# Attention and two feed-forward layers on one core: start-up loads, late coefficients and the planner's search changed together

## Chip, cores and metric

One core of a Trainium2 chip. The metric is the device time of one execution in microseconds; less is better.

## What is computed

Attention over 4 batches of 12 heads (448 positions, 64 wide), with q and k normalised by their root mean square and scaled by gains, then two feed-forward layers without a residual. The first has a cosine in it, the second a quotient of polynomials whose coefficients (moe2_a, moe2_b) are inputs.

```
q_n, k_n = rmsnorm(q, g_q), rmsnorm(k, g_k)
attn = softmax(q_n @ k_n.T / sqrt(64));  x = attn @ v        # -> 1792 tokens x 768
h = x @ w_in;   x = (h * cos(h)) @ w_out                     # 768 -> 2048 -> 768
h = x @ w_in2;  P = a0 + a1 h + a2 h^2 + a3 h^3;  Q = 1 + |b0||h| + |b1| h^2
out = (P / (Q + 1e-6)) @ w_out2
```

The weights (and a, b, and all else) arrive as 8-byte floats; the kernel takes the 4-byte value out of their bits itself.

## The kernel before, in words

**Work.** Heads go in pairs, 6 pairs per batch, 24 in all. For one pair, `att_load` loads k (three DMAs) and q (four) into the tile qk, `att_norm` squares, sums and scales them, `att_t` transposes both on PE (eight 128x128 matmuls against the identity) and copies them to kt and qt as a high and a low half; `att_s` makes the scores in four chunks (tiles t), of which DVE takes the maximum (mx) and ACT the exponential (e) with its sums; `att_vt` transposes e to et, and `att_va` multiplies et by v into x_ps. The inverse sums go to all partitions either through DRAM (rd, rb) or, in batch 0, by `att_rows`, which transposes broadcast columns on PE. The result x is again stored as high and low halves, since each fp32 product in the feed-forward layers is three single-pass products (hi hi, hi lo, lo hi).

A weight block of 768 KB is decoded by `decode`: a load (raw) on SP's queue, three passes on DVE (tiles w32), a copy on ACT (high half) and a subtraction on POOL (low half), then a store to DRAM (wd), from which `load_w` takes it later. Blocks in the list `early` are decoded ahead and only stored; the others are kept in the ring w as well.

**Stages.** Batch 0's attention runs alone up to about 105 us. Then, batch by batch, the first layer (tiles h_ps, the nonlinearity on tiles k and g in `act1`, the sum y) runs with the next batch's attention between its groups. In the last stage the second layer runs over all tokens.

**Order.** Nothing is scheduled on the chip. `Clock` is a model of the engines: `do` enters a task with an engine, a duration and the tasks that it needs; `step` starts tasks; `pe` advances the time of TensorE, in whose program order the kernel is written. `candidate` picks the next task of an engine by due time. Each of 40 rehearsals runs the kernel without emitting anything, and `plan` derives new due times from it; the best set is then used to emit the instructions. Within each engine they run strictly in the order in which they were emitted. Work outside the model (`gains`, `consts`, `coefficients`) is emitted where it is called.

All engine calls go through a recording helper, so nearly every row of the profile carries the line L293 (L330 in the changed kernel). Names of tiles tell the rows apart.

The `coefficients` call stands in `run` after batch 0's attention, directly ahead of the first nonlinearity:

```
            self.moe1_part(0, f, c, KD - 1 - c)
            self.h_done[0, f] = KD - 1
        self.coefficients(const_p)
```

Of the kernel before, what the change touches and what calls it, by code (L numbers as in the profile page):

```python
# [29 lines left out]
REHEARSALS = 40  # L30
EXP, SIN = "natural_log_exp_and_others", "trig_and_small"


class Task:
    __slots__ = (
        "eng", "fn", "prio", "tab", "size", "ready", "left", "succ", "end", "out", "n",
        "port", "parts", "name", "due", "need", "lst", "start",
    )


class Clock:
# [4 lines left out]
    READ, WRITE, WINDOW = 2.2, 1.5, 3.413  # L46
# [3 lines left out]
    def __init__(self, due=None):  # L50
        self.t, self.n, self.named = 0.0, 0, {}
        self.free = dict.fromkeys(("V", "A", "G", "S"), 0.0)
# [5 lines left out]
        self.window, self.half = [0, 0.0], True  # L58

    def do(  # L60
# [15 lines left out]
        k.due = self.due.get(k.name, math.inf) if self.due else None  # L76
        self.all.append(k)
# [19 lines left out]
    def enter(self, k):  # L97
        for e in k.eng:
            self.todo[e].append(k)

# [11 lines left out]
    def candidate(self, e):  # L112
# [4 lines left out]

        def ready(k):
# [3 lines left out]
            return max(k.ready, rival) if k.port else k.ready  # L122
# [16 lines left out]
    def step(self, until=math.inf):  # L139
        best = None  # L140
        for e in self.free:
            c = self.candidate(e)
# [7 lines left out]
        if eng == "S":  # L150
# [3 lines left out]
        if len(k.eng) > 1:  # L154
            k.fn(eng)
        else:
            k.fn()
# [7 lines left out]
        if k.size:  # L165
            lag = self.READ if k.size > 0 else self.WRITE
            self.dma = max(self.dma, end - k.eng["S"] / k.parts + lag) + abs(k.size)
# [4 lines left out]
            end += self.LATE  # L172
# [33 lines left out]
    def pe(self, dur):  # L206


        while dur > 1e-9:
            n = int(self.t // self.WINDOW)  # L210
            if n > self.window[0]:
                idle, part = n > self.window[0] + 1, self.window[1] / self.WINDOW
                self.half = idle or part < (0.62 if self.half else 0.5)
                self.window = [n, 0.0]
            rate = 0.53 if self.half else 1.0
            d = min(dur / rate, (n + 1) * self.WINDOW - self.t + 1e-6)
            self.window[1] += d
            self.t += d
            dur -= d * rate
# [100 lines left out]
class Kernel:  # L320
    def __init__(self, tc, a, due):
        self.tc, self.nc, self.a = tc, Engines(tc), a
        self.dry = isinstance(tc, Null)
        self.ck = Clock(due)
# [34 lines left out]
    def gains(self, c):  # L359
        nc, a = self.nc, self.a  # L360
        g2 = c.tile([P, 2], F32, name="g2")
        for i, n in enumerate(("g_q", "g_k")):
            for r in HALVES:
                nc.gpsimd.dma_start(out=g2[r, i : i + 1], in_=a[n].rearrange("(p o) -> p o", o=1))
        return g2

    def consts(self, c, g2):
        nc, a = self.nc, self.a
        ident = c.tile([P, P + SL], F32, name="ident")
        if not self.dry:  # L370
            make_identity(nc, ident[:, :P])
        nc.gpsimd.tensor_copy(ident[:, P:], ident[:, :SL])
        self.ident, self.swap = ident[:, :P], ident[:, SL:]
# [14 lines left out]
        nc.vector.scalar_tensor_tensor(self.gg, g2[:, 0:1], 0.125, g2[:, 1:2], ALU.mult, ALU.mult)  # L388

    def coefficients(self, c):  # L390
        nc, a = self.nc, self.a
        ab = c.tile([P, 6], F32, name="ab")
        nc.gpsimd.dma_start(out=ab[:, 0:4], in_=a["moe2_a"].partition_broadcast(P))
        nc.gpsimd.dma_start(out=ab[:, 4:6], in_=a["moe2_b"].partition_broadcast(P))
        self.na = c.tile([P, 4], F32, name="na")
        nc.vector.tensor_scalar(self.na, ab[:, 0:4], -1.0, None, ALU.mult)
        self.bb = c.tile([P, 2], F32, name="bb")
        nc.scalar.activation(self.bb, ab[:, 4:6], AF.Abs)
# [1008 lines left out]
```

## Time and profile before

| what | value |
|---|---|
| median of three runs | 1278.93 us (1273.4, 1278.93, 1279.43) |
| the profiled execution, own time | 1273.58 us |
| its span | 1271.8 us |
| PE busy | 1232.2 us, 97% |
| DVE, ACT, POOL busy | 68%, 56%, 22% |
| HBM traffic over the span | 221 GB/s |

The span runs from the first to the last instruction of the profile; the time of an execution lies around it. PE is TensorE's matmuls, DVE is VectorE, ACT is ScalarE, POOL is GpSimd, SP issues most DMAs. A row's idle time is that of its engine just before it, with what ended it. The granted clock (PEclk) is given as a share of 2.4 GHz, the higher of the two levels; 0.50 is 1.2 GHz.

### The profile page before, as it was taken

What the parts mean: (1) busy time and instruction counts of PE and PEld (TensorE: products, weight loads), DVE (VectorE), ACT (ScalarE), POOL (GpSimd) and SP (SyncE); (2) the same over time, 40 slices, a digit from 0 to 9 for tenths busy, and PEclk for the clock granted to TensorE, in tenths of its full rate; (3) what the DMA queues carried; (4) which work ended last, traced back from release to release, by engine and by line L of the source; (5) the groups of instructions that cost most, each with busy time, mean ns of one, the idle gap of its engine ahead of it and who ended that gap; (6) DMA issues with size and microseconds to landing.
All of it is one profiled execution on the core that took longest, in us unless ns stands there. A gap on an engine that the chain in (4) does not pass through costs nothing.

```text
span 1271.8 us, 18275 instructions
## 1 busy us (share of the span) xinstructions
PE 1232.2 (97%) x6624; PEld 1055.3 (83%) x6624; DVE 860.4 (68%) x1360; ACT 710.0 (56%) x1373; POOL 273.6 (22%) x356
## 2 busy tenths in 40 slices
PE   5988999899999998999999999999999999999998
PEld 3557777678877878877879999999999999999998
DVE  6986886965766856776846556775766676577663
ACT  6875776563766654666554324675544455554540
POOL 5654354440424231324112111100000000000000
PEclk9999999999999999999999999999999999999999
DMA  5778786887797689798589999713141825142312
GB/s 129 219 241 288 239 291 194 269 277 267 245 324 266 200 288 352 274 307 303 190 312 369 403 367 364 263 69 149 50 151 50 333 101 199 50 149 88 120 42 87
DMA packets 132266, 282.24 MB, mean 222 GB/s; under 512 B 57424, under 2 KB 90448, under 8 KB 132176
## 3 DMA queue, kind: packets, MB, share of 16 engines
q1 hardware_dynamic: 131984, 281.06, 62.7%
q8 instruction: 53, 0.87, 0.3%
q14 instruction: 37, 0.30, 0.1%
q0 software_dynamic: 192, 0.00, 0.0%
HBM read 214.11 MB, written 66.91 MB: 221 GB/s over the span
## 4 chain that ended last, share of the span: by engine, by line
PE 80%; DMA 4%; DVE 2%; ACT 1%; issue 1%; POOL 1%; SPq 0%; DVEq 0%; POOLq 0%; ACTq 0%
PE h_ps L293 48%; PE o_ps L293 18%; PE t L293 9%; PE x_ps L293 4%; DMA w<-wd 3%; DMA raw<-in_moe_w_in 1%; DVE w L293 1%; DVE k L293 0%; DMA rb<-rd 0%; ACT k L293 0%; POOL w L293 0%; ACT w L293 0%; DVE x L293 0%; ACT L293 0%; SPq L293 0%
## 5 line engine op out<-in xcount | busy, mean ns | idle before, releaser
L293 PE MATMUL h_ps<-x,w 128*128 128x448 f32 x2250 | 488.2, 370 | 8.9 <-DVE qt L293 3.8
L293 PEld LDWEIGHTS h_ps<-x,w 128*128 128x128 f32 x2250 | 419.5, 189 | 54.7 <-issue 12.0
L293 PE MATMUL h_ps<-g,w 128*128 128x448 f32 x1152 | 248.2, 369 | 8.1 <-DVE k L293 6.2
L293 PE MATMUL o_ps<-w,g 128*128 128x384 f32 x1344 | 244.7, 337 | 0.0
L293 PEld LDWEIGHTS h_ps<-g,w 128*128 128x128 f32 x1152 | 213.6, 188 | 34.3 <-DVE k L293 8.4
L293 PEld LDWEIGHTS o_ps<-w,g 128*128 128x128 f32 x1344 | 237.1, 188 | 1.9
L293 DVE SCALAR_TENSOR_TENSOR w<-raw,w 128x768 int32<-128x768 int32 x128 | 139.7, 1095 | 1.1
L293 ACT ACTIVATE e<-t,mx 128x448 f32<-128x448 f32 x168 | 105.3, 637 | 33.3 <-DVE mx L293 33.1
L293 POOL TENSOR_TENSOR raw<-w,raw 128x768 fp32r<-128x768 f32 x40 | 74.9, 1874 | 211.8 <-ACT raw L293 200.4
L293 DVE TENSOR_REDUCE mx<-t 128x1 f32<-128x448 f32 x168 | 94.9, 613 | 7.5 <-PE t L293 7.1
L293 PEld LDWEIGHTS t<-ident,e 128*128 128x128 f32 (+1 forms) x696 | 76.5, 138 | 24.6 <-issue 20.6
L293 ACT ACTIVATE et<-t 128x512 f32<-128x512 f32 (+1 forms) x168 | 82.2, 554 | 25.4 <-PE t L293 25.1
L293 PE MATMUL t<-kt,qt 64*128 64x448 f32 (+1 forms) x504 | 84.6, 406 | 5.6 <-ACT e L293 4.3
L293 PE MATMUL x_ps<-et,v 128*64 128x448 f32 (+1 forms) x384 | 89.2, 560 | 0.2 <-ACT et L293 0.2
L293 PE MATMUL t<-ident,e 128*128 128x128 f32 (+1 forms) x696 | 88.6, 277 | 0.0
L293 ACT ACTIVATE g<-q 128x448 fp32r<-128x448 f32 x64 | 36.9, 577 | 89.7 <-DVE q L293 89.6
L293 PEld LDWEIGHTS t<-kt,qt 64*128 64x128 f32 (+1 forms) x504 | 51.6, 194 | 35.8 <-issue 16.1
L293 DVE SCALAR_TENSOR_TENSOR k<-k,h_ps 128x448 f32<-128x448 int32 x61 | 37.7, 619 | 57.2 <-ACT k L293 56.9
L293 ACT ACTIVATE r<-v,cc 128x448 f32<-128x448 f32 x64 | 42.8, 669 | 48.7 <-DVE v L293 47.6
L293 ACT ACTIVATE q<-h_ps,na 128x448 f32<-128x448 f32 x64 | 46.4, 724 | 37.2 <-PE h_ps L293 36.3
L293 ACT ACTIVATE raw<-w 128x768 fp32r<-128x768 f32 x40 | 33.8, 847 | 58.0 <-DVE w L293 50.8
L293 DVE TENSOR_TENSOR q<-q,h_ps 128x448 f32<-128x448 f32 x64 | 39.7, 620 | 38.2 <-ACT w L293 36.1
(82 smaller groups left out, 1333.6 us busy)
## 6 DMA issues: line engine op xcount, KB each, us to landing
w<-wd SPq DMA_DIRECT2D x168, 768.0 KB
wd<-raw SPq DMA_DIRECT2D x40, 768.0 KB
raw<-in_moe_w_in SPq DMA_DIRECT2D x32, 768.0 KB
raw<-in_moe_w_out SPq DMA_DIRECT2D x32, 768.0 KB
wd<-w SPq DMA_DIRECT2D x24, 768.0 KB
xd<-x SPq DMA_DIRECT2D x24, 448.0 KB
x<-xd SPq DMA_DIRECT2D x24, 448.0 KB
out<-o SPq DMA_DIRECT2D x14, 384.0 KB
```

The costliest lines, as they stand in the source:

```text
L293: inst = fn(*args, **kw)
```

## The change

It has six parts.

- The coefficients' loads and their two small preparations become tasks of the model, entered early in batch 0. The gain vector gg becomes a task too, and its loads are two instead of four.
- Pair 0's loads are shared by SP's and ACT's queue. The identity is made ahead of the gain loads.
- q's and k's transposes are separate steps, each waiting for its own scaling.
- The inverse sums' rows are made by matmuls of half the array's columns each, into one tile, with one copy on ACT.
- v's tile gets a tail with zero rows, so the last product uses all 128 rows. From the third pair on, v is loaded once the pair two before has been multiplied.
- The planner: the model of TensorE's clock, a rule on the port that DVE and POOL share, four blocks instead of eight in `early`, and `polish`, a random search over the due times.

```
 def consts(self, c):
...
+        self.g2_load = self.ck.do("G", 1.03, lambda: self.gains(c), p=0, size=0.1, parts=2)
+        self.ck.emitted(self.g2_load)
...
+        self.gg_done = self.ck.do("V", 0.17, gain, self.g2_load, p=0)

 def coefficients(self, c):
-        nc.gpsimd.dma_start(out=ab[:, 0:4], in_=a["moe2_a"].partition_broadcast(P))
-        nc.gpsimd.dma_start(out=ab[:, 4:6], in_=a["moe2_b"].partition_broadcast(P))
-        nc.vector.tensor_scalar(self.na, ab[:, 0:4], -1.0, None, ALU.mult)
-        nc.scalar.activation(self.bb, ab[:, 4:6], AF.Abs)
+        def load():
+            nc.gpsimd.dma_start(out=ab[:, 0:4], in_=self.a["moe2_a"].partition_broadcast(P))
+            nc.gpsimd.dma_start(out=ab[:, 4:6], in_=self.a["moe2_b"].partition_broadcast(P))
+        k = ck.do("G", 1.15, load, p=2, size=3.0, parts=2)
+        ck.do("V", 0.17, lambda: nc.vector.tensor_scalar(na, ab[:, 0:4], -1.0, None, ALU.mult), k, p=2)
+        ck.do("A", 0.25, lambda: nc.scalar.activation(bb, ab[:, 4:6], AF.Abs), k, p=2)

 def att_load(self, b, j):
+            if first:
+                ka = ck.do("A", 0.65 * (2 - i), lambda load=load, ends=ends: load(ends[1 :: 2 + i], "scalar"), ...
+                ks = ck.do("S", 1.3, lambda load=load, ends=ends: load(ends[0::2]), ...

 def att_load_v(self, s):
-        v = s["v"] = self.at_p.tile([P, 2 * NM + 1, D], F32, tag="v", name="v", bufs=2)
+        v = s["v"] = self.at_p.tile([P, 2 * NC, D], F32, tag="v", name="v", bufs=2)
+        def blank():
+            for h, r in enumerate(HALVES):
+                nc.gpsimd.memset(v[r, 2 * NM + 1 - h], 0.0)

 def att_t(self, s):
-        ck.need(*s["kn"])
-        (tq, uq), (tk, uk) = (self.at_tile() for _ in range(2))
+        for i in (1, 0):
+            ck.need(s["kn"][1 - i])
+            self.att_t1(s, i)

 def att_va(self, s, kb):
-                v[:, h * NM + kb] if kb < NM else v[r, 2 * NM],
-                et[:, h * S : (h + 1) * S] if kb < NM else et[r, (1 - h) * SL :][:, :S],
+                v[:, h * NM + kb] if kb < NM else v[:, 2 * NM + h],
+                et[:, h * S : (h + 1) * S] if kb < NM else et[:, (1 - h) * SL :][:, :S],
...
+            n = s["b"] * NJ + s["j"] + 2
+            if n in self.st:
+                self.att_load_v(self.st[n])

 def att_rows(self, s):
-                nc.tensor.transpose(
-                    tp[:, a : a + P], s["sm"][:, k : k + 1].to_broadcast([P, P]), self.ident[:]
-                )
+                nc.tensor.matmul(
+                    t[r, a : a + i.stop - i.start],
+                    s["sm"][:, c : c + 1].to_broadcast([P, D]),
+                    self.ident[:, i],
+                    start=True, stop=True,
+                )

 def run(self):
-        early = (...)[7:15]
+        early = (...)[7:11]
...
         take(cur, 8)
+        self.coefficients(const_p)
...
-        self.coefficients(const_p)

+def polish(due):
+    rng = random.Random(SEED)
+    ck = rehearse(due)
+    where = {k.name: k.at for k in ck.all}
+    for s in range(len(ck.at)):
+        best = (rehearse(due, s + AHEAD).at)[-1]
+        for _ in range(MOVES):
+            width = rng.choice(WIDTHS)
+            new = {
+                n: t + rng.gauss(0, width) if s <= where[n] < s + SPAN else t for n, t in due.items()
+            }
+            got = rehearse(new, s + AHEAD).at[-1]
+            if got < best - 0.02:
+                due, best = new, got
+    return due
```

Since the planner's model and its search change, instructions move on all engines. Three places are shown here; the number at the end of a tile's name is the buffer's number, and the two kernels number their buffers differently.

First, ACT from the start of the program, before (qk_110 and qk_127 are pairs 0 and 1, sq their squares, r0 their inverse roots, kt and qt the copies of the transposes):

```order
L293 ACT_TABLE_LOAD
L293 ACTIVATE sq_151<-qk_110 128x512
L293 ACTIVATE r0_129<-ss_128,cc_117 128x8
L293 ACTIVATE r0_129<-r0_129,cc_117 128x8
L293 ACTIVATE sq_160<-qk_110 128x512
L293 ACTIVATE r0_129<-ss_128,cc_117 128x8
L293 ACTIVATE r0_129<-r0_129,cc_117 128x8
L293 ACTIVATE sq_172<-qk_127 128x512
L293 ACTIVATE sq_197<-qk_127 128x512
L293 ACTIVATE kt_190<-t_180 128x448
L293 ACTIVATE qt_189<-t_179,gg_124 128x512
```

and in the change, where qk_102 and qk_134 are pairs 0 and 1:

```order
L330 DMA qk_102<-in_k 128x3x64
L330 DMA qk_102<-in_q 128x3x64
L330 DMA qk_102<-in_q 64x64
L330 ACT_TABLE_LOAD
L330 ACTIVATE sq_147<-qk_102 128x512
L330 ACTIVATE r0_136<-ss_135,cc_126 128x8
L330 ACTIVATE r0_136<-r0_136,cc_126 128x8
L330 ACTIVATE sq_160<-qk_102 128x512
L330 ACTIVATE r0_136<-ss_135,cc_126 128x8
L330 ACTIVATE r0_136<-r0_136,cc_126 128x8
L330 ACTIVATE sq_187<-qk_134 128x512
L330 ACTIVATE kt_143<-t_168 128x448
```

Three DMAs of pair 0 now stand at the head of ACT, in front of its table load; behind it the order is the same, but for pair 1's second square, which no longer stands in front of the copy kt.

Second, ACT where batch 0's first nonlinearity begins, before (raw is a decoded block, k the tiles of the nonlinearity, bb the second coefficient):

```order
L293 ACTIVATE rb_1354<-t_1329 64x448
L293 ACTIVATE rb_1354<-t_1330 64x448
L293 ACTIVATE x_1347<-rb_1354 128x448
L293 ACTIVATE raw_1287<-w32_1357 128x768
L293 ACTIVATE bb_1418<-ab_1413 128x2
L293 ACTIVATE k_1425<-h_ps_997,cc_117 128x448
L293 ACTIVATE raw_1368<-w32_1411 128x768
L293 ACTIVATE k_1431<-h_ps_1032,cc_117 128x448
L293 ACT_TABLE_LOAD
```

in the change at the same place:

```order
L330 ACTIVATE rb_1348<-t_1324 128x448
L330 ACTIVATE raw_1227<-w32_1335 128x768
L330 ACTIVATE x_1338<-rb_1348 128x448
L330 ACTIVATE raw_1247<-w32_1346 128x768
L330 ACTIVATE k_1412<-h_ps_987,cc_126 128x448
L330 ACTIVATE k_1418<-h_ps_1009,cc_126 128x448
L330 ACT_TABLE_LOAD
L330 ACTIVATE k_1412<-k_1412,cc_126 128x448
```

and in the change where bb now stands, during the attention of pairs 1 and 2 (e are exponentials, et copies of their transposes):

```order
L330 ACTIVATE e_369,sums1_65<-t_358,mx_370 128x448
L330 ACTIVATE et_391<-t_375 128x512
L330 ACTIVATE et_391<-t_376 128x384
L330 ACTIVATE kt_399<-t_401 128x448
L330 ACTIVATE qt_398<-t_408,gg_133 128x512
L330 ACTIVATE et_429<-t_414 128x512
L330 ACTIVATE et_429<-t_415 128x384
L330 ACTIVATE bb_333<-ab_331 128x2
```

The coefficient's row has left the place in front of the first k, and one block's copy has left the place between the first two k.

Third, DVE at the turn from the first layer's nonlinearity to the scores of the pair of heads that comes next in batch 0's third group, before (w32 are decode passes, mx the maxima of the scores):

```order
L293 TENSOR_TENSOR k_2693<-h_ps_2660,k_2693 128x448
L293 TENSOR_SCALAR w32_2733<-raw_2639 128x768
L293 TENSOR_SCALAR w32_2736<-raw_2685 128x768
L293 SCALAR_TENSOR_TENSOR w32_2733<-raw_2639,w32_2733 128x768
L293 SCALAR_TENSOR_TENSOR w32_2736<-raw_2685,w32_2736 128x768
L293 SCALAR_TENSOR_TENSOR w32_2733<-raw_2639,w32_2733 128x768
L293 SCALAR_TENSOR_TENSOR w32_2736<-raw_2685,w32_2736 128x768
L293 TENSOR_TENSOR g_2692<-k_2693,g_2692 128x448
L293 TENSOR_TENSOR y_1532<-h_ps_2721,y_1532 128x448
L293 TENSOR_REDUCE mx_2769<-t_2752 128x1
L293 TENSOR_REDUCE mx_2769<-t_2753 128x1
```

and in the change:

```order
L330 TENSOR_TENSOR kt_2698<-t_2699,kt_2698 128x448
L330 TENSOR_TENSOR g_2661<-k_2668,g_2661 128x448
L330 SCALAR_TENSOR_TENSOR qt_2697<-t_2705,gg_133,qt_2697 128x512
L330 TENSOR_TENSOR k_2695<-h_ps_2670,k_2695 128x448
L330 TENSOR_TENSOR y_1519<-h_ps_2722,y_1519 128x448
L330 TENSOR_REDUCE mx_2759<-t_2750 128x1
L330 TENSOR_REDUCE mx_2759<-t_2751 128x1
L330 TENSOR_REDUCE mx_2775<-t_2761 128x1
L330 TENSOR_REDUCE mx_2775<-t_2760 128x1
```

Six decode passes stood between k's product and the maxima; in the change there are none there.

## Rows read from the trace of the kernel before

**Rows 1.** The page: span, busy time by engine, shares of the chain that ended last.
```profile
span 1271.8 us, 18275 instructions
...
PE 1232.2 (97%) x6624; PEld 1055.3 (83%) x6624; DVE 860.4 (68%) x1360; ACT 710.0 (56%) x1373; POOL 273.6 (22%) x356
...
PE 80%; DMA 4%; DVE 2%; ACT 1%; issue 1%; POOL 1%; SPq 0%; DVEq 0%; POOLq 0%; ACTq 0%
```

**Rows 2.** Timeline from 0 to 20 us: start us, duration us, what, [idle before <-releaser].
```profile
0.74 2.02 SPq L293 DMA_DIRECT2D qk<-in_k  x3
...
4.78 0.63 ACT L293 ACTIVATE sq<-qk 128x512 f32<-128x512 f32 x1 [2.77 <-POOL qk L293]
...
5.95 0.16 DVE L293 SCALAR_TENSOR_TENSOR gg<-g 128x1 f32<-128x1 f32 x1 [4.94 <-DMA g<-in_g_k]
...
6.03 0.68 DVE L293 TENSOR_REDUCE ss<-sq 128x8 f32<-128x512 f32 x1
...
9.27 1.11 PE L293 MATMUL t<-ident,qk 128*128 128x128 f32 x4 [9.27 <-DVE qk L293]
...
19.10 2.12 PE L293 MATMUL t<-ident,qk 128*128 128x128 f32 x8 [2.27 <-POOL qk L293]
```

**Rows 3.** Timeline near 73 us, PE.
```profile
73.03 1.49 PE L293 MATMUL h_ps<-x,w 128*128 128x448 f32 x3 [3.81 <-DVE qt L293]
```

**Rows 4.** Stretches: busy us (x) of PE, PEld, DVE, ACT, POOL; PEclk, DMA, GB/s.
```profile
40.00:50.00 10.00, 10.00 (x64) 6.04 (x63) 9.78 (x15) 9.55 (x24) 4.91 (x6) 1.00 0.75 208
...
73.00:76.00 3.00, 2.96 (x12) 2.40 (x12) 3.00 (x5) 1.63 (x3) 0.64 (x2) 0.50 0.99 385
...
123.40:129.00 5.60, 5.58 (x21) 5.06 (x22) 4.89 (x9) 4.97 (x9) 1.84 (x1) 0.70 1.02 402
```

**Rows 5.** Timeline from 113 to 129 us: ACT and PE round the coefficients.
```profile
113.94 1.38 PE L293 MATMUL h_ps<-x,w 128*128 128x448 f32 x6
...
118.36 0.20 ACT L293 ACTIVATE bb<-ab 128x2 f32<-128x2 f32 x1 [7.89 <-DMA ab<-in_moe_b]
...
118.59 0.64 ACT L293 ACTIVATE k<-h_ps,cc 128x448 int32<-128x448 f32 x1
...
123.42 5.47 PE L293 MATMUL h_ps<-x,w 128*128 128x448 f32 x18 [3.24 <-DVE k L293]
```

**Rows 6.** Timeline near 884 us, PE: 18 matmuls of the same kind.
```profile
883.86 3.88 PE L293 MATMUL h_ps<-x,w 128*128 128x448 f32 x18 [0.73 <-DMA w<-wd]
```

**Rows 7.** Timeline from 237 to 246 us: PE, DVE and ACT.
```profile
237.51 1.11 DVE L293 TENSOR_SCALAR w<-raw 128x768 int32<-128x768 int32 x2
...
237.60 0.47 PE L293 MATMUL h_ps<-g,w 128*128 128x448 f32 x1 [1.23 <-POOL w L293]
...
238.54 3.54 DVE L293 SCALAR_TENSOR_TENSOR w<-raw,w 128x768 int32<-128x768 int32 x4
...
241.25 1.77 ACT L293 ACTIVATE w<-w 128x768 fp32r<-128x768 f32 x2 [3.04 <-DVE w L293]
...
243.08 2.20 DVE L293 TENSOR_REDUCE mx<-t 128x1 f32<-128x448 f32 x4
...
245.11 0.88 PE L293 MATMUL t<-kt,qt 64*128 64x448 f32 x5 [2.60 <-ACT e L293]
```

**Rows 8.** Timeline near 480 us: DVE and PE.
```profile
479.66 0.56 DVE L293 TENSOR_SCALAR w<-raw 128x768 int32<-128x768 int32 x1 [3.18 <-DMA raw<-in_moe_w_in]
...
480.81 1.49 PE L293 MATMUL h_ps<-g,w 128*128 128x448 f32 x6 [3.23 <-DVE k L293]
```

**Rows 9.** Timeline near 81 us, PE: one group of sum rows and what follows.
```profile
81.02 1.09 PE L293 MATMUL t<-ident,sums 128*128 128x128 f32 x8
...
82.03 0.97 PE L293 MATMUL x_ps<-et,v 64*64 64x448 f32 x4
```

**Rows 10.** Timeline near 12 us, POOL: three memsets of one pair.
```profile
11.92 0.58 POOL L293 MEMSET qk<- 64x128 f32 x3 [6.27 <-PE t L293]
```

**Rows 11.** Waits: who for whom, us in total, times, longest us.
```profile
DVE w L293 <- DMA raw<-in_moe_w_in: 13.3, 8, 4.4
```

More of the change, by code (lines that the diff above doesn't have):

```diff
@@ L57, in __init__ @@
         self.due, self.all, self.count = due, [], {}
-        self.window, self.half = [0, 0.0], True
+        self.form = ""
+        self.share, self.half, self.last = 0.0, True, 0.0
+        self.work, self.at, self.limit, self.dry = 0.0, [], limit, dry
+        self.stale, self.next = set(), dict.fromkeys(self.free)
     def do(
@@ L99, in enter @@
             self.todo[e].append(k)
+            self.stale.add(e)
+        if k.port:
+            self.stale.update("VG")
     def has(self, *tasks):
@@ L116, in candidate @@
         rival = self.port["G" if e == "V" else "V"] if e in "VG" else 0.0
+        o, near = {"V": "G", "G": "V"}.get(e), []
+        if self.due and o:
+            near = [
+                (u.due, max(u.ready, self.free[o]), u.eng[o])
+                for u in self.todo[o]
+                if u.port and (len(u.eng) == 1)
+            ]
+            near.sort(key=lambda x: x[1])
         def ready(k):
@@ L121, in ready @@
                 return max(k.ready, self.dma - self.QUEUE)
-            return max(k.ready, rival) if k.port else k.ready
+            if not k.port:
+                return k.ready
+            r = max(k.ready, rival)
+            for due, ru, du in near:
+                at = max(r, self.free[e])
+                if due < k.due and at < ru + du and at + k.eng[e] > ru + 0.1 and k.due > ru + du:
+                    r = ru + du
+            return r
         start = max(self.free[e], min(map(ready, todo)))
@@ L204, in settle, with pe @@
             pass
[L206 to L219, printed above, removed]
+    def pe(self, dur, form=""):
+        if form != self.form:
+            self.form, dur = form, dur + 0.09
+        keep = math.exp((self.last - self.t) / self.WINDOW)
+        self.share *= keep
+        self.half = self.share < (0.62 if self.half else 0.5)
+        self.work += dur
+        dur /= 0.53 if self.half else 1.0
+        self.t += dur
+        self.last = self.t
+        self.share = 1 - (1 - self.share) * math.exp(-dur / self.WINDOW)
+        while len(self.at) * self.STEP <= self.work:
+            self.at.append(self.t)
+            if len(self.at) >= self.limit:
+                raise Stop
         while self.step(self.t - self.AHEAD):
@@ L1233, in run @@
         self.at_ring = Ring(7, make)
-        g2 = self.gains(const_p)
         load(0)
-        self.consts(const_p, g2)
+        ck.emitted(*chain.from_iterable(s[1:] for s in st[0]["load"].values()))
         self.act_set(EXP)
+        self.consts(const_p)
         load(1)
@@ L1372, in run, with rehearse @@
         self.close(*[p for p, _ in self.open[::-1]])
+def rehearse(due, limit=math.inf):
+    dry = Kernel(Null(), Null(), due, limit)
+    try:
+        dry.run()
+    except Stop:
+        pass
+    return dry.ck
+def polish(due):
[13 more added lines that the diff above has]
+    return due
 @with_exitstack
 def body(ctx: ExitStack, tc: tile.TileContext, a):
+    gc.disable()
     due, best = None, (math.inf, None)
     for _ in range(REHEARSALS):
-        dry = Kernel(Null(), Null(), due)
-        dry.run()
-        best = min(best, (dry.ck.t, due), key=lambda x: x[0])
-        due = dry.ck.plan(due)
-    Kernel(tc, a, best[1]).run()
+        ck = rehearse(due)
+        best = min(best, (ck.t, due), key=lambda x: x[0])
+        due = ck.plan(due)
+    due = polish(best[1])
+    gc.enable()
+    Kernel(tc, a, due).run()
 def kernel(**inputs):
```

213 lines of the change are left out of this document (116 added, 97 removed).

## Prediction

> **What bounds the kernel now.** I read the page's busy shares first, then the chain that ended last, then TensorE's own row of time for every place where it sat idle, then what stood in the queues of the engine it waited for. TensorE is busy for 1232.2 us of a span of 1271.8 [rows 1], and the chain runs through PE for 80% of the span. So an edit is worth what it takes out of the 39.6 us in which PE sat idle, plus what PE loses to its lower clock after an idle stretch. Of the idle time 9.27 us lie before the first matmul [rows 2]; the other stretches named below come to 2.27 + 3.81 + 3.24 + 1.23 + 2.60 + 3.23 = 16.4 us [rows 2, 3, 5, 7, 8]. In each of them the reader is to see the same thing: DVE and ACT take their instructions strictly in the planner's order, and one that is not ready holds up the one that PE needs.
>
> **The change, part by part.** The terms are set against the profiled execution, 1273.58 us.
>
> *Start.* The three k loads of pair 0 take SP 2.02 us, 0.67 each [rows 2]. With one of them on ACT, the last k load is issued one step sooner: a gain of 0 (the transfers were the limit) to 0.67. DVE's gg waits for the POOL loads until 5.95, and the reduce behind it starts at 6.03, though its square ended at 4.78 + 0.63 = 5.41. The change puts gg behind the reduce: 0.6. Three of pair 0's seven loads leave SP, so pair 1's loads start up to 3 x 0.67 = 2.0 sooner, and it is pair 1 that PE waits for before 19.10 (2.27 idle). At that place the gain lies between 0.6 (gg alone) and 3.5 (0.67 + 0.6 + 2.27). I take 2.5, nearest to pair 1's 2.0 with gg's 0.6. ACT's three issues stand ahead of its table load, where ACT had 2.77 us idle before its first square [rows 2]. That covers three issues at SP's 0.67; were it gone, up to 2.0 would come back. Two queues do not widen a transfer, by the Trainium skill, "DMA: Bandwidth & Descriptors", section "Rules for kernel authors": spreading loads over the issuing engines only saves issue time. By that rule the 0.67 could shrink to nothing and the term would be 1.8; by the row, where loads are spaced by their issues, it stands.
>
> *Transposes of k and q apart.* PE idles 3.81 us before 73.03, waiting for DVE's qt [rows 3], and runs the next 3 us at a granted clock of 0.50, its lower level [rows 4], half of which, 1.5, is lost. The split lets each copy be queued behind its own transposes. But decode passes still stand on DVE near there, so of 0 to 5.3 I take 1.0.
>
> *Coefficients.* This is the largest term. ACT stands 7.89 us before bb, waiting for a load issued only then [rows 5]. Behind bb stands the first k at 118.59, while the last six matmuls for the two h tiles began at 113.94 and took 1.38. So k could have started near 115.3, 3.3 sooner. PE waits 3.24 us for that chain's product, then needs 5.47 for 18 matmuls, at a granted clock of 0.70 in that stretch [rows 4]; 18 such matmuls later take 3.88 [rows 6]. The price of the wait is 3.24 + 1.59 = 4.8. In the change bb and na run long before, and ACT comes from the last attention copies straight to k (the second place shown above). From 0 (the wait only moves to the attention stage) to 4.8, I take 4.8: 3.3 sooner covers 3.24 of idle time, and without the idle stretch the clock has no cause to fall. If the new loads land late, bb and na hold up the softmax instead. bb now stands behind a whole stretch of exponentials and copies of later tiles (last rows of that place), and that is its cover.
>
> *The new order around the decode.* At 237.5 to 242 DVE runs six decode passes of two blocks in a row (1.11 + 3.54 us), and ACT their two copies, before the maxima that four exponentials wait for; PE idles 1.23 us before 237.60 and 2.60 before 245.11 [rows 7]. In the change none of the six stand there (the third place). Out of 0 to 3.8 I take 3.2: the 2.60 whole, since DVE would reach the maxima 4.65 sooner, and half of the 1.23, which is the wait for a weight and hangs on where the decode went. At 479.66 one decode pass waited 3.18 us for its raw load with k's product behind it, and PE stood 3.23 [rows 8]. Whether the new order still meets a late load there cannot be read with confidence; out of 0 to 3.2 I take half, 1.6.
>
> *Sum rows by half-array matmuls.* Eight transposes took 1.09 us [rows 9]. Nearest to the new form are the column-halved x_ps matmuls beside them: four of 448 columns took 0.97, so at 128 columns four steps take 4 x 0.97 x 128/448 = 1.1. I take 0. If the halves did not overlap it would be 2.2, and six such groups cost 6.6 in all. Below, I see no more than the 0.12 between 1.09 and 0.97, 0.7 in all. The tail of v by zero rows streams as many columns as before: nothing on PE.
>
> *Added on POOL:* 48 memsets, 0.58/3 = 0.19 each [rows 10], 9.3 us on an engine that is 22% busy; 0 while that cover holds. Four blocks fewer are written and reloaded early; DMA is not what PE mostly waited for, so 0.
>
> *Given back.* The decode passes that leave those places stand elsewhere, and four blocks move from the first attention stage to later. A new stall of the kind in rows 8 costs 3.2. From 0 to 9 (three of them) I take 2.1, about two thirds of one. Late next, where a stall goes, are the k tiles of the first FFN groups.
>
> **Sum:** -2.5 - 1.0 - 4.8 - 3.2 - 1.6 + 2.1 = -11.0 us. That gives 1262.6 against the profiled 1273.58. The median of the runs shown is 1278.93, and they lie at 1273.4 and near 1279. I set the sum against the mean of the three runs and the profiled one, 1276.3, and forecast **1265**.
>
> **Rivals.**
> - *PE was not the bound where I saved.* In the attention stage of batch 0 DVE and ACT are nearly as full as PE (9.78 and 9.55 of 10 us from 40 us on [rows 4]), so what the start saves may be lost to them, and new stalls may eat two of the three large terms. For it: DVE's and ACT's 68% and 56% busy [rows 1] hide that full early stage. Against it: the waits named in the rows are for loads and misplaced passes, not for lack of engine time. The coefficients alone would stay, less three tenths of a stall: 1276.3 - 4.8 + 1 = about 1272.5, between 1270 and 1277. Chance 0.18.
> - *Half-array matmuls don't overlap.* +6.6 on the forecast: 1271.6. Against it: two column halves of 448 columns share 0.97 us in rows 9. The Trainium skill, "TensorEngine Tiling (Array Packing)", section "Restrictions", says that column tiling rules out the transpose mode for fp32 input, so these are full matmuls where transposes stood. The trace agrees only in part: x_ps shows the price of full matmuls, but no row has one with 128 columns. Chance 0.06.
> - *Slower: DVE's queue behind raw loads.* A denser plan asks for decode passes just when it thinks the load lands. Each one that lands late holds DVE, as at 479.66, for 3.2 us, and PE with it. With a gross gain of 13.1, it takes seven such stalls to be slower by over 0.5%; eight give 1276.3 - 13.1 + 25.6 = 1289. For it: the DMA engines' share is 0.99 and 1.02 in two early stretches [rows 4]. Against it: before, all eight waits of that kind for moe_w_in come to 13.3 us, the longest 4.4 [rows 11]. Chance 0.08.
> - *The plan changes nothing that counts.* Then 1276. The three places shown above speak against it. Chance 0.02.
>
> **How the numbers follow.** The forecast (1256 to 1270) has 0.66. Faster or slower counts from 0.5%, about what a measurement of this kernel can tell from no change: under 1272.5, over 1285.3. Faster: 0.66 + 0.06 + a third of the first rival = 0.78. Same: its other two thirds and the last rival, 0.14. Slower: 0.08. The range reaches from 1254 (a run at 1273.4, nothing given back, start, coefficients and both decode places at their upper ends, and 4.1 of the split's 5.3: 3.5 + 4.8 + 3.8 + 3.2 + 4.1 = 19.4) up to 1277, where the first rival ends. That leaves out the slower case and the far ends.
>
> **What would show it.** In the profile after: no ACT wait for ab above 1 us and no PE idle stretch of 3 us before the first h tile's release; the granted clock at 1.0 in the 6 us behind; the second pair's transposes near 16.6 instead of 19.10; maxima directly behind y's add where the six decode passes stood, and no 2.60 wait before that pair's scores. PE's idle time should be near 29 instead of 39.6 with PE's busy time lower by one or two. It is wrong if PE's idle time stays near 40 with the gaps elsewhere, if the sum-row groups take 2 us instead of 1.1, or if DVE's waits for raw loads come to more than 30 us.

## The result, and the profile after

The changed kernel takes 1246.55 us (median of four runs, 1246.05 to 1247.34); the kernel before took 1278.1 on the same chip (four runs, 1273.4 to 1279.43). The ratio is 0.976 (95% interval 0.9734 to 0.9786): 31 us faster, where 11 were forecast. Between the profiled executions it is 27.3 us (1273.58 to 1246.33). The other 4 lie in the runs: before's profiled execution was among its fastest, after's was an ordinary one.

The page of the changed kernel (first lines and the chain), against [rows 1]:

```profile
span 1244.5 us, 18447 instructions
...
PE 1220.6 (98%) x6672; PEld 1052.9 (85%) x6672; DVE 847.4 (68%) x1359; ACT 712.4 (57%) x1375; POOL 267.1 (21%) x395
```

PE's idle time fell from 39.6 to 23.9 us (15.7), and its busy time from 1232.2 to 1220.6 (11.6). The forecast saw about 10 of the first and "one or two" of the second. PE issues the same matmuls in the same order in both kernels, the sum rows apart. So the start of the n-th matmul can be compared, and each stretch credited with what it gained:

| up to the start of | before | after | gained | forecast |
|---|---|---|---|---|
| the second pair's transposes | 19.10 | 16.97 | 2.1 | 2.5 |
| the transposes ahead of the first h tile | 67.61 | 63.62 | 1.9 | 0 |
| the x_ps behind the first h tile | 75.95 | 66.39 | 5.6 | 1.0 |
| an x_ps in mid-stage | 104.42 | 93.86 | 1.0 | 0 |
| the transposes behind the 18 matmuls that waited for the coefficients | 128.72 | 113.06 | 5.1 | 4.8 |
| the next group's transposes | 140.10 | 123.17 | 1.3 | 0 |
| the first product with w_out ahead of the six decode passes | 233.26 | 217.06 | -0.7 | 0 |
| the transposes behind the six decode passes | 245.92 | 224.54 | 5.2 | 3.2 |
| a transpose of e between the two decode places | 458.68 | 435.55 | 1.7 | 0 |
| the matmuls behind the late raw load | 480.81 | 454.54 | 3.1 | 1.6 |
| the last 168 matmuls | 1237.55 | 1210.52 | 0.8 | -2.1 |

The places were right. The first h tile gave more than five times its term, the five stretches with no term gave 5.2 together, and at the end nothing had been given back: the one stretch that lost anything lost 0.7. The rows of PE at these places in the changed kernel (start us, duration us, what, [idle before <-releaser]), against [rows 2, 3, 5, 7, 8]:

```profile
16.97 2.12 PE L330 MATMUL t<-ident,qk 128*128 128x128 f32 x8 [0.70 <-POOL qk L330]
...
64.83 0.88 PE L330 MATMUL h_ps<-x,w 128*128 128x448 f32 x3
...
109.42 3.81 PE L330 MATMUL h_ps<-x,w 128*128 128x448 f32 x18
...
217.06 2.70 PE L330 MATMUL h_ps<-g,w 128*128 128x448 f32 x12 [1.23 <-DVE k L330]
...
223.73 0.88 PE L330 MATMUL t<-kt,qt 64*128 64x448 f32 x6
...
454.54 3.71 PE L330 MATMUL h_ps<-g,w 128*128 128x448 f32 x17 [0.37 <-DVE k L330]
```

The waits of 3.81, 3.24, 2.60 and 3.23 us are gone or down to 0.37; the 1.23 for a weight is gone as well, while the wait for k at the first product with w_out grew from 0.63 (before 233.26) to 1.23. Stretches of the changed kernel at the first h tile and at the 18 matmuls (columns as in [rows 4]):

```profile
64.80:67.80 3.00, 2.98 (x16) 1.99 (x17) 3.00 (x5) 3.00 (x6) 1.05 (x1) 1.00 0.33 70
...
109.40:113.10 3.70, 3.70 (x20) 3.37 (x20) 2.41 (x5) 2.96 (x5) 2.04 (x2) 1.00 1.01 412
```

The granted clock is 1.00 in both, where it was 0.50 and 0.70.

### The profile page after: what moved, and what is told of

Its sections match the earlier page's. It is cut to its first block, busy times and chain, and to the rows that moved or that the text cites. A ratio compares the mean times of both kernels' runs of the same rounds, so it can differ in the third digit from the quotient of the medians.

```text
span 1244.5 us, 18447 instructions
## 1 busy us (share of the span) xinstructions
PE 1220.6 (98%) x6672; PEld 1052.9 (85%) x6672; DVE 847.4 (68%) x1359; ACT 712.4 (57%) x1375; POOL 267.1 (21%) x395
## 4 chain that ended last, share of the span: by engine, by line
PE 84%; DVE 5%; DMA 4%; ACT 3%; issue 2%; POOL 1%; SPq 0%; POOLq 0%; ACTq 0%; DVEq 0%
PE h_ps L330 49%; PE o_ps L330 18%; PE t L330 11%; PE x_ps L330 5%; DMA w<-wd 3%; DVE w L330 2%; DMA raw<-in_moe_w_in 1%; DVE k L330 1%; ACT k L330 1%; DVE mx L330 1%; DMA wd<-w 1%; ACT e L330 1%; SPq L330 0%; ACT w L330 0%; POOL qk L330 0%
## 5 line engine op out<-in xcount | busy, mean ns | idle before, releaser
L330 DVE SCALAR_TENSOR_TENSOR w<-raw,w 128x768 int32<-128x768 int32 x128 | 126.8, 1000 | 1.1
L330 POOL TENSOR_TENSOR raw<-w,raw 128x768 fp32r<-128x768 f32 x36 | 66.8, 1856 | 159.8 <-ACT raw L330 141.1
L330 PEld LDWEIGHTS t<-ident,e 128*128 128x128 f32 (+1 forms) x696 | 75.7, 137 | 24.5 <-issue 16.9
L330 PE MATMUL x_ps<-et,v 128*64 128x448 f32 x384 | 85.8, 554 | 0.7 <-ACT et L330 0.7
L330 POOL TENSOR_TENSOR w<-w,w 128x768 fp32r<-128x768 f32 x28 | 56.0, 2006 | 59.6 <-ACT w L330 52.9
```

What stands on the lines that cost most here:

```text
L330: inst = fn(*args, **kw)
```

## The experiments

The question was what made 31 of 11. The **repairs** theory: two long waits of PE (first h tile, coefficients) were worth far more than their terms. The **plan** theory: the new order, through the search and the refitted model, made most of it. "Plan held" below means that every due time and the order on each engine stay those of the changed kernel; the traces of e2, x1, z1, z2 and z5 show that order on ACT, DVE and POOL, but for the coefficients where they are moved.

### Score banks turned, in the kernel before (e8) and in the changed one (e3)

The idle time before 73.03 was put down to qt, but the matmul there does not read qt. The first h tile takes two banks of PSUM from the ring of seven that transposes and scores use in turn. In the kernel before, 77 tiles had been taken by then, a multiple of 7, and the two banks held the newest transposes of k and q, which DVE had not yet read. The new sum rows take one tile where the old took two. That makes 74, and the banks hold finished scores. So each kernel was given the other's banks by starting its ring some places later:

```
-        turn, at_n = iter_tiles([at_ps] * 5 + [early_ps] * 2), [0]
+        turn, at_n = iter_tiles([at_ps] * 5 + [early_ps] * 2, 2), [0]     # e8; 3 in e3
...
```

Measured: e8 1282.08 us (ratio 1.0033, 1.0007 to 1.0059), e3 1254.62 (0.9823, 0.9802 to 0.9843). They were expected to do this:

> The kernel before with one edit: the ring of seven PSUM banks starts two banks later, so the two banks that the first h tile takes over hold two e transposes instead of pair 5's k and q transposes. Theory 'banks': PE's 3.81 us wait before the first h matmul and the lower clock behind it go; PE's lead over before at the matmuls behind it is 3 to 5.6 us, end about 1269 to 1274. Theory 'search': the wait goes only with the new planner; lead under 1 us there.

> The changed kernel with one edit: its ring starts three banks later, so that the first h tile takes over the banks of the newest k and q transposes, as in the kernel before. Theory 'banks': a PE wait of 1.5 to 4 us comes back before the first h matmul, 2 to 5.6 us lost there, end 1249 to 1252. Theory 'search': the search orders ACT and DVE round it; under 1 us lost, end 1246.5 to 1247.5.

What idled PE ahead of the h tile between 64 and 78 us, counted for the weight load and the matmul alike; first the kernel before, then e8:

```profile
L293 PE MATMUL h_ps<-x,w x5: 363/575/741, 73.0 to 77.9; 128*128 128x448 f32 x5
its engine sat idle before it (us, times) until:
  DVE qt L293: 7.9, 2
```

```profile
L293 PE MATMUL h_ps<-x,w x6: 361/364/447, 67.5 to 71.1; 128*128 128x448 f32 x6
its engine sat idle before it (us, times) until:
who waited for it (us, times):
```

In e8 the wait is gone with the old, joined transposes; the stretch from the transposes ahead of the tile to the x_ps behind it gains 5.4 us, where it gained 5.6 in the changed kernel. In e3 the wait is back with the new, split ones (PE idle 2.98 us before 68.69). So it is the bank, not the split. But e8 lost all of it again, and did not end at the 1269 to 1274 that the bank theory expected: 5.6 us went at the coefficients and the rest in the new plan. (e3, too, ended later than its 1249 to 1252.) At the coefficients it was partly the load itself: ACT waited 11.48 us, and the second load landed 9.0 us after its issue, where it had taken 5.4 in the kernel before. The issue before, then the issue, ACT and PE in e8 (for the landing before, see [rows 5]):

```profile
112.95 0.54 POOL L293 DMA_DIRECT2D ab<-in_moe_b  x1
```

```profile
109.84 0.54 POOL L293 DMA_DIRECT2D ab<-in_moe_b  x1
...
118.84 0.20 ACT L293 ACTIVATE bb<-ab 128x2 f32<-128x2 f32 x1 [11.48 <-DMA ab<-in_moe_b]
...
123.80 2.61 PE L293 MATMUL h_ps<-x,w 128*128 128x448 f32 x6 [8.35 <-DVE k L293]
```

### Coefficients: late in the changed kernel, plan held (e2), as tasks in the kernel before (e5)

```
         k = ck.do("G", 1.15, lambda: None, p=2, size=3.0, parts=2)        # e2: load, na and bb
...
             self.h_done[0, f] = KD - 1
+        if not self.dry:
+            self.coef_late()
```

> The changed kernel with its plan held, but the coefficients' two loads and two small instructions are issued where the kernel before has them, ahead of the first nonlinearity. Theory 'coefficients': ACT waits 3 to 8 us for bb there again, PE stands over 2.5 us, 4.8 to 6.6 us are lost, end 1251 to 1253, and the runs scatter more than the changed kernel's 1.3 us, since the landing of these loads varies. Theory 'search': with the new plan there is slack; under 2 us lost.

> The kernel before with one edit: the coefficients as tasks of the model, entered where the change enters them; planned by the 40 rehearsals of before. Theory 'coefficients': PE's 3.24 us wait at 123 and the clock loss behind it go, lead 4.8 to 6.6 us at the first groups of the first layer, end near 1268 to 1272. Theory 'search': the new stalls of the old planner take most of it back, lead under 2 us at the end.

Measured: e2 1255.04 us (0.9834, 0.9814 to 0.9853), e5 1283.75 (1.0058, 1.004 to 1.0077). In e2, the second load's issue, ACT and PE where the coefficients are used:

```profile
104.49 0.56 POOL L330 DMA_DIRECT2D ab<-in_moe_b  x1
...
112.64 0.20 ACT L330 ACTIVATE bb<-ab 128x2 f32<-128x2 f32 x1 [10.66 <-DMA ab<-in_moe_b]
...
116.59 6.35 PE L330 MATMUL h_ps<-x,w 128*128 128x448 f32 x18 [7.57 <-DVE k L330]
```

The 18 matmuls take 6.35 us for 3.81: they start 7.2 later than in the changed kernel, and 2.5 goes to the lower clock (0.50 in the first 3 us, 0.66 in the next 3.5), of which 1.2 comes back. The load landed 8.1 us after its issue here; issued at 20.63, as in the changed kernel, it landed after 3.0. In e5 the same repair gained 5.0 at its place, 4.8 having been forecast. But the planner had also put a later pair's squares and sums ahead of the et that x_ps waits for (PE idle 2.23 before 35.86), and the end came 6 us later than before, worse than either theory expected.

### Both repairs in the kernel before (e9)

Edits of e8 and e5 together. Measured: 1278.15 us (1.0, 0.9989 to 1.0012).

> The kernel before with both repairs, the score banks turned by two tiles and the coefficients as tasks at the start; old planner and old clock, no search. Structure (the waits stand in series, and each repair alone was eaten by the next wait): about 1265 to 1270, faster than before and than either alone. Search (a repair is given back unless the plan is made anew for it): 1275 or more, as either alone was.

The repairs theory missed here. Both waits are gone (74.01 and 119.70 start without one): the two stretches gain 4.7 and 5.0. But 4.3 had been lost ahead of them, most of it at 35 us, so that at 123.35 the kernel is 5.4 ahead, and 4.2 of that goes by 139, where new waits stand and 12 matmuls take 4.46 us that take 2.70 in the kernel before. By 250 us the lead is gone.

```profile
35.63 1.35 PE L293 MATMUL x_ps<-et,v 128*64 128x448 f32 x4 [2.24 <-ACT et L293]
...
132.52 4.46 PE L293 MATMUL h_ps<-g,w 128*128 128x448 f32 x12
```

Under the old planner a repaired wait was given back.

### The search: taken out (e1), put into the kernel before (e6), another seed (x4), twice the moves (x5)

```
-    due = polish(best[1])
+    due = best[1]                                   # e1
-SEED, MOVES, SPAN, AHEAD, WIDTHS = 3, 6, 3, 8, (0.5, 1.0, 2.0, 4.0)
+SEED, MOVES, SPAN, AHEAD, WIDTHS = 4, 6, 3, 8, (0.5, 1.0, 2.0, 4.0)    # x4; 3, 12 in x5
```

> The changed kernel without the jittered rehearsals: the planner's 40 rehearsals and its new clock model stay, and so do the bank rotation, the early coefficients, the two queues for pair 0 and the half-array sums. Structure (banks and coefficients make the gain, the random search little): about 1248 to 1254, and the steps at the first h and before 123 us stay whole. Search (the jittered rehearsals make most of the gain after 130 us and keep the rest from being given back): above 1258, with the loss growing steadily after the first stage.

> The kernel before with the jittered rehearsals added and nothing else (its own clock model, banks, coefficients, queue and sums). Search: at or below 1268, the gain spread over the decode places. Structure: 1273 or more, since the waits at the first h (3.8 us) and at the coefficients (4.4 us) stay and the search cannot move either.

> The changed kernel with another seed for the jitter and nothing else, to learn how much of any difference is the luck of one plan. If the search as such makes the gain, within 3 us of 1246.5. If the seed was a lucky one, 1250 to 1258, and then the 8 us that the kernels with turned banks and with eight early blocks lost are no larger than the luck of a plan, and only their steps in the trace can be put down to their edits.

> The changed kernel with 12 jittered moves a step where it has 6. If the search still has something to find: 1240 to 1245. If PE's idle time is used up (23.9 us, of it 9.2 before the first matmul): 1245 to 1250. If each search is a draw of luck as between the two seeds (1246.5 and 1252.3): anything up to 1254.

Measured: e1 1257.79 us (0.9846, 0.982 to 0.9872), e6 1283.75 (1.0047, 1.0029 to 1.0065), x4 1252.26 (0.9807, 0.9787 to 0.9827), x5 1248.62 (0.9782, 0.9755 to 0.9809). The search is worth 11 us in the changed kernel with its seed, 5.5 with another, and less than nothing in the kernel before. In e1 the loss grows to 5 us by 134 and 9.5 by 464, and no further. More moves found nothing better, and no run beat the changed kernel. The 6 us between the two seeds is taken as what one plan's luck is worth. So a run that was planned anew is read by its steps in the trace, and prices come from runs with the plan held.

### The old clock model, with the search (x2) and without (x3)

```
-                if due < k.due and at < ru + du and at + k.eng[e] > ru + 0.1 and k.due > ru + du:
-                    r = ru + du
...
-        ck.pe(0.76, "columns")
+        ck.pe(0.948)
```

The rule for TensorE's clock is put back too, and is not shown here.

> The changed kernel, jittered rehearsals and all, planned by the clock model of before (its rule for TensorE's clock, its costs for scores and x_ps, no rule that keeps POOL and DVE apart, all engines free from 0). Model theory (what the repairs left is made by a planner that knows the durations better, and the search can only follow its model): 1260 or more. Search theory (the search finds its gain under either model): 1252 or less.

> The same old clock model and no jittered rehearsals: only the repairs, the two queues for pair 0 and the matmul forms are new. It splits the 20 us between the kernel before with both repairs (1278.2) and the changed kernel without the search (1257.8). Forms and start alone are worth 2.7 + 1.2 + 2.1 = 6: if the model makes the rest, 1268 to 1275; if forms and start set off more than their own cost, 1262 or less.

Measured: x2 1258.23 us (0.9855, 0.9836 to 0.9873), x3 1263.44 (0.9889, 0.9865 to 0.9913). So the model alone gave 5.6 (x3 to e1), the search alone 5.2 (x3 to x2), and both together 16.9. With the other seed it is 11, about their sum. Each of the first two is no larger than one plan's luck, so only the two together are shown to be worth something. x2 lies between its two expectations, nearer the model's. x3 also fell between, so the edits outside the planner are worth more than the 6 us that it allowed them: 14.7 from e9 to x3, of which some 6 could be luck. One thing that the plan changes is seen in DVE's decode passes, first in x2, then in the changed kernel (count | busy us, mean ns | idle before):

```profile
L316 DVE SCALAR_TENSOR_TENSOR w<-raw,w 128x768 int32<-128x768 int32 x128 | 145.8, 1142 | 1.2
```

```profile
L330 DVE SCALAR_TENSOR_TENSOR w<-raw,w 128x768 int32<-128x768 int32 x128 | 126.8, 1000 | 1.1
```

The same 128 passes take 19 us less in the plan made by the new model, which keeps POOL's and DVE's work apart. That this rule is the cause is not shown: without the search the two models differ by 3.9 us (137.5 in x3, 133.6 in e1), and with the other seed it is 130.9.

### Eight early blocks in the changed kernel (e7)

```
-        early = (...)[7:11]
+        early = (...)[7:15]
```

> The changed kernel with eight score blocks instead of four taken early, which moves the rotation of the score banks by four tiles again and puts score work ahead of the first h. If only the tile that the first h takes counts, it keeps its bank free or not by that count alone: 1246 to 1252 if free, about 1255 (as with the banks moved back) if the first h waits for the newest transposes again. If the length of the early list itself matters, slower than 1256.

Measured: 1254.18 us (0.9813, 0.9792 to 0.9834). The decoded blocks take no tile of the ring, so the count stays at 74 and the banks are not turned, other than expected. The first h tile does not wait, so the lower figure was due, and it came out 2 us above it. The loss is spread over 80 to 180 us, and is no larger than luck allows. What the four blocks are worth stays open.

### v's tail in quarters again, plan held (x1)

```
-                v[:, h * NM + kb] if kb < NM else v[:, 2 * NM + h],
-                et[:, h * S : (h + 1) * S] if kb < NM else et[:, (1 - h) * SL :][:, :S],
+                v[:, h * NM + kb] if kb < NM else v[r, 2 * NM + h],
+                et[:, h * S : (h + 1) * S] if kb < NM else et[r, (1 - h) * SL :][:, :S],
```

> The changed kernel with its plan held and one matmul form put back: v's tail is multiplied as 64-row quarters of the array again, not as whole columns over zero rows. The traces have 8 x_ps matmuls at 1.80 us with such a tail and at 1.66 without, and 18 of 24 tails stand in such groups: 18 x 0.14 = 2.5. Forms theory (the tail's form is worth something on PE): 1248 to 1250.5. Zero theory (as many columns stream, nothing on PE): 1246.5, within 0.7.

Measured: 1250.73 us (0.9798, 0.9777 to 0.9819), 4.2 more. Between the profiled executions it is 3.7, of which 3.5 lies at the 24 tails, about 0.15 at each: 0.10 on the step from the matmul ahead to the first quarter (0.37 to 0.47 where x_ps stands ahead) and 0.05 inside the tail. Waits moved but took nothing in sum: the 1.23 before 217.06 is gone, and 0.70 and 0.48 stand before 228.91 and 229.85, with a lower clock behind them. One group of eight x_ps matmuls and the row behind it, in x1 and in the changed kernel:

```profile
334.64 1.87 PE L330 MATMUL x_ps<-et,v 128*64 128x448 f32 x8
336.44 1.75 PE L330 MATMUL t<-ident,e 128*128 128x128 f32 x14
```

```profile
336.90 1.72 PE L330 MATMUL x_ps<-et,v 128*64 128x448 f32 x8
338.56 1.64 PE L330 MATMUL t<-ident,e 128*128 128x128 f32 x13
```

From start to start it is 1.80 us with a tail of 64-row quarters, 1.66 with the zero rows.

### Banks, one queue, and four edits undone, plan held (z1, z2, z5)

The banks are turned without telling the planner (z1: the offset of e3 only where the kernel is emitted), pair 0 is loaded from SP alone (z2), and both of these with e2's and x1's edits (z5):

```
-        turn, at_n = iter_tiles([at_ps] * 5 + [early_ps] * 2), [0]
+        turn, at_n = iter_tiles([at_ps] * 5 + [early_ps] * 2, 0 if self.dry else 3), [0]
...
-                ka = ck.do(... load(ends[1 :: 2 + i], "scalar") ...
+                ka = ck.do(... load(ends[1 :: 2 + i], "sync") ...
```

> The changed kernel, plan held: the tiles for scores and transposes take their banks three places later in the ring, but the planner is not told, so the order of all instructions stays and only the bank behind the first h tile differs (it holds the newest transposes of k and q again). Bank theory: the first h waits some 3 us for qt and then runs 1.4 slower at the lower clock: 1250.5 to 1252.5. If the whole loss of the run with turned banks (8.1) was the bank: 1254 or more. If it was only the new plan: 1247 or less.

> The changed kernel, plan held: pair 0's loads of k and q are all issued by SP again. Start theory of the prediction (three issues of 0.67 are taken off SP's queue ahead of pair 1): the second pair's transposes come 1.5 to 2.5 later and the time is 1248 to 1249. If the start's gain came from gg behind the reduce and the gain loads alone, or if PE makes it up later: 1247 or less.

> The changed kernel, plan held, with four edits undone together: banks turned back, coefficients at the old place, v's tail in 64-row quarters, one queue for pair 0. If the prices add (bank 4 to 5, coefficients 8.5, tail 4.2, queue 0 to 2): 1263 to 1266. If the first two stand in series and one wait hides in the other: 1257 to 1261. What is left to 1277 is what order and rehearsals give without them.

Measured: z1 1252.27 us (0.9805, 0.9772 to 0.9838), z2 1249.39 (0.9788, 0.9762 to 0.9814), z5 1264.27 (0.9905, 0.9875 to 0.9934). PE at the first h tile, in z1 and then in z5, where the 18 matmuls behind the coefficients follow:

```profile
67.69 0.87 PE L330 MATMUL h_ps<-x,w 128*128 128x448 f32 x3 [2.82 <-DVE qt L330]
```

```profile
68.82 0.97 PE L330 MATMUL h_ps<-x,w 128*128 128x448 f32 x3 [2.82 <-DVE qt L330]
...
122.74 6.08 PE L330 MATMUL h_ps<-x,w 128*128 128x448 f32 x18 [7.10 <-DVE k L330]
```

Of z1's 5.7, 2.7 is lost at the h tile, with no loss of clock behind it, 1.4 near 230 us and the rest mostly later. Near 230 PE waits 0.69 and 0.47 for qt and kt before the scores, as it does in x1 and in e2, whose banks are not turned; so this part isn't shown to belong to the bank. Of z2's 2.8 only 0.5 is lost at the start, where 1.5 to 2.5 was expected. The rest is lost at 177 us, where PE then waits 1.61 for qt and 0.81 for kt (0.57 in the changed kernel), and nothing ties that to the queue.

So the prices with the plan held are 5.7 (bank), 8.5 (coefficients), 4.2 (tail) and 2.8 (queue). They sum to 21.2, and undone together they cost 17.7. The sum is too high because the single runs hold losses at other places. Read at their own places, bank, coefficients, tail and queue lose 2.7, 9.0, 3.5 and 0.5 us in the single runs, 15.7 together, and 4.3, 8.5, 3.5 and 0.7 in z5, which is 17.0 of the 18.5 between the profiled executions. The queue's 2.8 is not clear of noise: z2's ratio and the changed kernel's lie 0.0028 apart, and each is known to 0.0026. What is left to the kernel before, 1276.4 - 1264.3 = 12.1, is the planner with the smaller edits, not taken apart further. Both theories hold a part, and neither works alone.

## Why the prediction was wrong, point by point

**The view of the whole held**: PE bounds the kernel, and an edit is worth what it takes out of PE's idle time and its lower clock. The range failed because terms were taken at or near 0 that were not: the split's 1.0 (5.6 measured), the tail's 0 (about 3.5), and the 2.1 for new stalls, in place of which stretches without a term gained.

**"Start ... I take 2.5"**: 2.1 was gained, but not for the reason given, that pair 1's loads start up to 2.0 sooner. In z2 they are issued at 5.15 as before (5.16), and the second pair's transposes come at 17.49, only 0.5 later; the other 1.6 does not come from the queue. Nor did the last k load or gg bring anything: the first reduce starts at 5.89 instead of 6.03, held now by a later square, and the first matmul at 9.18 instead of 9.27. What held them in the kernel before was POOL, behind and beside two decode passes of DVE. These rows of the kernel before I had not read:

```profile
14.66 0.56 DVE L293 TENSOR_SCALAR w<-raw 128x768 int32<-128x768 int32 x1 [0.28 <-DMA raw<-in_moe_w_in]
...
15.26 0.96 DVE L293 SCALAR_TENSOR_TENSOR w<-raw,w 128x768 int32<-128x768 int32 x1
15.36 0.93 POOL L293 TENSOR_TENSOR t<-r 128x16 f32<-128x16 f32 x1
...
17.20 0.95 DVE L293 SCALAR_TENSOR_TENSOR w<-raw,w 128x768 int32<-128x768 int32 x1
...
17.32 2.72 POOL L293 TENSOR_TENSOR qk<-qk,r 128x512 f32<-128x512 f32 x2
```

And POOL in the changed kernel, with no decode pass beside it:

```profile
14.62 0.22 POOL L330 TENSOR_TENSOR t<-r 128x16 f32<-128x16 f32 x1
...
15.87 2.04 POOL L330 TENSOR_TENSOR qk<-qk,r 128x512 f32<-128x512 f32 x2
```

POOL's small product takes 0.22 instead of 0.93, and the two scalings start 1.45 sooner. The Trainium skill, "SBUF — State Buffer", section "Who interferes with whom", says that a DVE instruction with two SBUF inputs contends with POOL instructions that read SBUF. The trace agrees: the decode pass with two inputs is the one beside the slow product. The scalings gain too, 2.04 for 2.72, and the second such pass stands beside them in the kernel before.

**"Transposes of k and q apart ... I take 1.0"** is the step that failed first. 5.6 were gained there, the upper end of 5.3 and a little more. The row said "<-DVE qt", and I read it as a wait for the data of qt. e8 shows that the split has no part in it: the bank had to come free. Nothing in the part on the change speaks of the ring's tiles, and a change from two tiles to one in `att_rows` was costed only by its matmuls.

**"Coefficients ... I take 4.8"** was right in mechanism and nearly in size: 5.1 in the ledger. e2 prices the same wait at 8.5 in the changed kernel. There PE ran out of work 7.0 us after ACT had begun to wait, 9.7 in the kernel before, and the load landed 8.1 us after its issue instead of 5.4. Why it landed so late in some runs is open.

**"The new order around the decode", 3.2 and 1.6**, gave 5.2 and 3.1. The place at 480 took the whole of its range, so no late load was met. Of the first, 3.1 came where the 2.60 stood and 2.1 ahead of it, more than the 1.23 that I had seen there; against that, 0.7 was lost just before, at the wait for k.

**"Sum rows by half-array matmuls ... I take 0"**: they overlap better than the x_ps row let me expect. One group in the changed kernel and the row behind it, against [rows 9]:

```profile
45.13 0.99 PE L330 MATMUL t<-ident,sums 128*64 128x128 f32 x16
45.95 0.92 PE L330 MATMUL x_ps<-et,v 128*64 128x448 f32 x4
```

From start to start the 16 take 0.82, where the 8 transposes took 82.03 - 81.02 = 1.01: six groups give 1.1 us. The greater worth of the edit is the tile that it no longer takes, which turned the banks. That the new count ended on free banks is luck: another count could have ended on the newest tiles again, as e3 does.

**"The tail of v by zero rows streams as many columns as before: nothing on PE"** failed: x1 prices it at 4.2, of which 3.5 is seen at the tails. Columns were the wrong measure: two thirds of the cost is on the step into the quarters, where the form changes, the rest inside them. The Trainium skill, "TensorEngine Tiling (Array Packing)", section "Key Properties", says that a change of the tiling mode drains the array. The trace agrees: the zero rows keep x_ps in one form, and about 0.15 us goes from every tail.

**"Given back ... I take 2.1"**: in sum nothing was. The runs point to the planner: the search and the new model together are worth 11 to 17 us (x3 against x4 and the changed kernel), while under the old planner two repairs were given back whole (e9). I had costed `polish` and the model only through the places where the order differed. DVE's waits for moe_w_in, on which the rival "DVE's queue behind raw loads" rested, fell from the 13.3 of [rows 11] to 2.2; those for moe_w_out rose from 3.7 to 6.5.

**The rival "PE was not the bound where I saved"** did not come true in the changed kernel. But something like it is what e8, e5 and e9 did in the kernel before. There new stalls ate the repairs: at 35 us in the early stage (e5, e9), at the coefficients' load (e8), and from 130 us on in all three, behind that stage. **"Half-array matmuls don't overlap"** fell: 0.82 us, not 2.2.

## What to carry to other kernels

A wait named by a tile can be a wait for that tile's memory: ask what the waiting instruction writes, count the tiles of the ring up to there, and see whose buffer it takes; an edit that takes one tile more or less turns all later ones. In a kernel whose order a planner makes, a repair alone may show nothing, since the next plan gives it back: price an edit with the plan held, read the price at the edit's own place in the trace, and measure another seed before believing a difference of a few microseconds. And look at the form of small matmuls before their columns: a quarter-array tail behind half-array matmuls cost about 0.15 us each time, with no idle time to show it.

## What the runs showed of the hardware that was not expected

- **Equal waits, unequal clocks.** In z1 and z5 PE idles 2.82 us at the same matmul. The next 3 us ran at a granted clock of 1.00 in z1 and 0.61 in z5, behind the same work, and at 0.50 in e3 after 2.98. So what an idle stretch of this length cost in clock was anywhere from nothing to 1.6 us (z5 loses 4.3 at this place, z1 2.7). Stretches of z1, then of z5:

```profile
67.60:70.60 3.00, 2.91 (x16) 1.93 (x17) 0.63 (x2) 1.17 (x3) 1.62 (x4) 1.00 1.00 368
```

```profile
68.80:71.80 3.00, 2.98 (x12) 2.21 (x14) 0.56 (x1) 0.41 (x2) 1.55 (x4) 0.61 0.99 372
```

- **With two queues the first load came later.** With pair 0's loads on two queues the first square starts at 5.23, waiting 1.30 for k; from one queue (z2) it starts at 4.46, when k has landed. q's square comes at 7.15 against 7.65, and what the second queue gave at the first matmul is 0.5 us (9.18 against 9.70). The Trainium skill, "DMA: Bandwidth & Descriptors", section "Issuing engines are not separate DMA queues", says that DMAs of several issuers run on the same engines and interleave. The trace agrees so far as it goes: the runs show when the squares start, not the transfers themselves. The first square in the changed kernel, then in z2:

```profile
5.23 0.63 ACT L330 ACTIVATE sq<-qk 128x512 f32<-128x512 f32 x1 [1.30 <-DMA qk<-in_k]
```

```profile
4.46 0.63 ACT L330 ACTIVATE sq<-qk 128x512 f32<-128x512 f32 x1 [2.44 <-POOL sums L330]
```

- **The same small load landed after 3.0 to 9.0 us.** The second coefficient load took 3.0 us from its issue at 20.63 in the changed kernel, and 5.4, 7.9, 8.1 and 9.0 where it is issued late (the kernel before, z5, e2, e8). So its landing is part of the price of issuing it where it is needed. Both loads from issue to landing, in the changed kernel and then in e8:

```profile
DMA to landing us min/median/max: 3.0/3.0/3.1
```

```profile
DMA to landing us min/median/max: 6.2/7.6/9.0
```
